# Products of scores and signs on GpSimd that wait for VectorE's mask, in a newly fitted order of work

## The chip, the cores and the metric

The kernel runs on one NeuronCore of one Trainium2 chip. The metric is the time of one execution on the device in microseconds (us). The engines are named as in the profile: PE is TensorE, DVE is VectorE, ACT is ScalarE, POOL is GpSimd, SP is SyncE, which issues the transfers.

## What is computed

A top-32 attention (8 batches, 8 heads, 576 tokens, head size 64) is followed by a layer of three products with a maximum over them and an output product (4608 tokens, 512 to 768 to 512), all in float32:

```python
scores = scale * np.matmul(q, k.transpose(0, 1, 3, 2))
kth = np.partition(scores, -top_k, axis=-1)[..., -top_k:-top_k + 1]
mask = scores >= kth
scores = np.where(mask, scores, -1000000000.0)
scores = scores - np.max(scores, axis=-1, keepdims=True)
attn = np.exp(scores)
attn = attn / (np.sum(attn, axis=-1, keepdims=True) + 1e-09)
attn_out = np.matmul(attn, v)
x = attn_out.transpose(0, 2, 1, 3).reshape(B * S, H * D)
h = np.maximum(np.maximum(x @ w1, x @ w2), x @ w3)
out = h @ w_out
```

## The kernel before

**Attention.** It goes by 144 units, each 128 queries for a pair of heads (t = 0 and 1), so that most steps come twice a unit, 288 times in all. PE makes the scores (`qk`, L508) and ACT moves them to SBUF (`evac`, L516, tile `ssb`, 128x576 for each t). To find the 32nd largest score of a row, DVE takes the eight largest of seven parts of it (`sweep`, L525), and the steps of `pivot` (L539 to L557) make from these a bound Q close to it; between them POOL turns a copy over (`negate`, L531). ACT writes the sign of Q minus score into a tile `w` and counts (`sign`, L564). POOL multiplies scores by these signs in place (`window`, L569, called the product below), DVE takes the eight largest of the result (`below`, L573), and POOL and DVE pick the threshold from the count (`place` L580 and L582, `leave` L586, `pick` L591). The mask on DVE (`mask`, L614) compares scores with the threshold and subtracts, reading `ssb` twice and writing it, and ACT takes the exponential (`expo`, L623). POOL and DVE make the inverse sum (`denominator` L629, `inverse` L633), ACT widens it (`widen`, L638), PE turns the result (`turn`, L664 to L669), ACT moves it (`turned`, L681), PE multiplies by the values (`values`, L700), and DVE, ACT and POOL scale the sums and split them into a high and a low half-precision part (`scaled_x` L710, `high_x` L724, `low_x` L728). These are x, the input of the MLP.

**The MLP.** It runs by spans of tokens: two a batch (0 to 256 and 256 to 576), three in the first. For each span and each of six blocks f, PE makes three sums (`layer`, L757, 12 matmuls each), ACT scales the first (L764), DVE takes the running maximum for the other two (`largest`, L766), ACT and POOL split it (L769, L772), and PE makes the output from all blocks (`layer2`, L817). Before that, the weights are loaded, decoded on DVE (L254 to L260), and cut into high and low parts by PE and ACT (`cut`, L325 to L334); the scale `rises` (L305) is ready when all of w1 to w3 have been seen.

**What sets the order.** Each engine works through its own list of instructions in the order in which the program issues them. That order is made by `in_order` (lines 71 to 131) at build time. Every step is a `Piece` with an engine, a cost, the pieces it needs, and a rank (its unit's number plus an offset by its kind, from the table `OFFSETS`). MLP steps are a second list, `fill`, which PE takes up when no ranked piece can start sooner, within limits of patience (`PATIENCE`) and of keeping PE in one mode (`SWITCH`, `STICK`; the modes are "rows" for `qk`, "columns" for `values`, none for the rest). Pieces marked `alone` (mask, fourth pivot step, weight decoding) share something with POOL: the planner puts them and POOL's pieces apart by its own clock:

```python
if x.alone:
    t = max(t, free["POOL"] + LOCK_A)
elif x.engine == "POOL":
    t = max(t, shut[0] + LOCK_B)
```

On the chip nothing keeps mask and product apart: the product's own needs are the sign and the buffer.

Of the kernel before, what the change touches and what calls it, by code (L numbers as in the profile page):

```python
# [14 lines left out]
ALU = mybir.AluOpType  # L15
# [9 lines left out]
NSSB = 5  # L25
NWB = 6
PMB = 2
GAP = 67.0
NEAR = 182.0
SWITCH = 100.0  # L30
STICK = 204.0
WINDOW = 150
LEAD = 49.1
LOCK_A = -150.0
LOCK_B = -100.0
OFFSETS = {'E0': -2.08, 'E1': -11.9, 'E2': 1.81, 'N': -19.09, 'T0': 7.0, 'T1': 7.99, 'T2': 7.02, 'Y': -1.5, 'Z': -8.28, 'd':
# [9 lines left out]
RANK_M = -20.0  # L46
LATE = {'PE': 160.0, 'DVE': 85.0, 'ACT': 100.0, 'POOL': 40.0, 'SP': 2000.0}

# [82 lines left out]
        left -= 1  # L131


PATIENCE = {'PE': 162, 'DVE': 131, 'ACT': 0, 'POOL': 85, 'SP': 0}


@with_exitstack
def kernel(ctx, tc, q, k, v, moe_w1, moe_w2, moe_w3, moe_w_out, out):
    nc = tc.nc
    B, NP, _, S = q.shape  # L140
    D = v.shape[-1]
    P = 128
    C = S // 64
    NU = S // P
    DM, DF = moe_w1.shape
    DO = moe_w_out.shape[1]
    KC = DM // P
# [63 lines left out]
    CUTS = {DF: DF // 2, DO: DO}  # L211
# [144 lines left out]
    lows = {}  # L356
# [47 lines left out]
    wo_scaled, wi_scaled = [], []  # L404
# [156 lines left out]
    def sign(n, t):  # L561

        d = st[n]
        nc.scalar.activation(d["w"][t], d["ssb"][t], AF.Sign, bias=d["Q"][:, t, 0:1], scale=-1.0, accum_out=d["cnt"][:, t:t + 1])  # L564

    def window(n, t):

        d = st[n]
        nc.gpsimd.tensor_tensor(d["w"][t], d["ssb"][t], d["w"][t], ALU.mult)  # L569

    def below(n, t):
        d = st[n]
# [37 lines left out]
    def mask(n, t):  # L610

        d = st[n]
        ss = d["ssb"][t]
        nc.vector.scalar_tensor_tensor(ss, ss, d["kth"][:, t:t + 1], ss, ALU.is_lt, ALU.subtract,  # L614
                                       accum_out=d["lost"][:, t:t + 1])

    def expo(n, t):
        d = st[n]
# [115 lines left out]
    def mlp(b, first, spans, tiles, alone, needs, rank):  # L734
# [39 lines left out]
        for c0, c1 in spans:  # L774
# [3 lines left out]
            for f in range(FC):  # L778
                box, prev, before = {}, None, []
                for i in range(3):  # L780
                    rel = []
                    for kcs in ((0, 1), (2, 3)):
                        x = add("PE", 6 * max(0.434 * w, 64.0), lambda i=i, f=f, kcs=kcs, c0=c0, c1=c1, box=box: layer(i, f, kcs, c0, c1, box),
                                [*needs, *(lows[i * KC + kc, f * P // CUTS[DF] * CUTS[DF]] for kc in range(KC) if lows)],
                                [("m", rel)] if kcs[0] == 0 else [])
                    now = []
                    y = add("DVE" if i else "ACT", 85 + 1.2 * w if i else 125 + 0.97 * w, lambda i=i, w=w, box=box: largest(i, w, box),
                            [x, *prev] if i else [x, *wi_scaled], [("h1", now)])
                    rel.append(y)
                    if i:  # L790
                        before.append(y)
                    before, prev = now, [y]
# [362 lines left out]
```

## Time and profile before

| | us |
|---|---|
| median of 3 runs (1251.45 to 1253.36) | 1251.83 |
| profiled execution, its own time | 1251.33 |
| span of the profiled execution | 1249.5 |
| outside the span | 1.8 |
| PE busy, share of the span | 1158.7, 93% |
| DVE busy | 1141.2, 91% |
| ACT busy | 1036.4, 83% |
| POOL busy | 866.0, 69% |
| mean granted PE clock | 0.976 |

The page gives busy time by engine and the chain of work that ended last; windows give the same by stretch, which separates the start (weights are decoded, little MLP work can run), the long middle, and the end (only MLP work is left). A granted clock of 1.00 is 2.4 GHz, 0.5 is 1.2 GHz.

### The profile page before, as it was taken

Reading aid. Unit: us, or ns where it says so; the run is one execution under the profiler, and the core shown is the slowest. Engines: PE = TensorE matmul, PEld = TensorE weight load, DVE = VectorE, ACT = ScalarE, POOL = GpSimd, SP = SyncE. Lnnn points to the kernel's source line nnn. Section 1 sums busy time; section 2 is a strip of 40 time slices with the busy share of each in tenths; the row PEclk is TensorE's granted clock in tenths of the full one; section 3 lists DMA queues with packets and bytes.
Section 4 is the critical chain, followed back from the end, with each engine's and each line's share of the span. In section 5 each row is a group of like instructions: output and inputs, shape, how many; then the busy total and the mean of one; then the engine's idle time right before and its main releaser. Section 6 shows DMA issues by size and latency. Waiting matters only on the chain.

```text
span 1249.5 us, 30550 instructions
## 1 busy us (share of the span) xinstructions
PE 1158.7 (93%) x9891; PEld 839.8 (67%) x9891; DVE 1141.2 (91%) x5547; ACT 1036.4 (83%) x2406; POOL 866.0 (69%) x1293
## 2 busy tenths in 40 slices
PE   4677789998999999999999999999899999999997
PEld 2355568775776757676777768666676768776764
DVE  8999898999999999999999999999999999999511
ACT  3688899898789998899889998898888988998621
POOL 5456687876677787777787778767777777877410
PEclk9788899999899999999999999999899999999999
DMA  8440111100111011100111021101011010000000
GB/s 329 130 139 1 56 40 48 39 28 23 36 40 47 11 55 28 58 11 20 47 48 39 11 64 40 37 11 39 29 39 47 11 47 19 13 7 2 18 18 29
DMA packets 33864, 54.74 MB, mean 44 GB/s; under 512 B 12960, under 2 KB 12960, under 8 KB 33696
## 3 DMA queue, kind: packets, MB, share of 16 engines
q1 hardware_dynamic: 33696, 52.71, 13.5%
q8 instruction: 80, 1.31, 0.4%
q14 instruction: 88, 0.72, 0.2%
HBM read 43.25 MB, written 9.44 MB: 42 GB/s over the span
## 4 chain that ended last, share of the span: by engine, by line
PE 61%; DVE 27%; ACT 8%; issue 2%; POOL 1%; DMA 0%; ACTq 0%; DVEq 0%; POOLq 0%
PE m L757 26%; PE tr L700 9%; PE s L508 9%; PE tr L669 7%; DVE L L525 7%; PE m L817 6%; DVE ssb L614 5%; DVE Q L573 4%; ACT pm L623 2%; ACT w L564 2%; PE tr L664 2%; DVE h L766 1%; DVE z L554 1%; ACT ssb L516 1%; ACT pT L681 1%
## 5 line engine op out<-in xcount | busy, mean ns | idle before, releaser
L569 POOL TENSOR_TENSOR w<-ssb,w 128x576 f32<-128x576 f32 x288 | 432.0, 1506 | 62.0 <-ACT w L564 58.8
L757 PE MATMUL m<-xh,wall 128*128 128x256 f16 (+3 forms) x2448 | 438.4, 279 | 5.8 <-DVE h L766 3.2
L757 PEld LDWEIGHTS <-wall 128*128 128x128 f16 x3672 | 347.3, 98 | 82.5 <-issue 13.5
L757 PE MATMUL m<-xl,wall 128*128 128x256 f16 (+3 forms) x1224 | 339.0, 279 | 0.0
L525 DVE MAX8 L<-ssb 128x8 f32<-128x82 f32 (+1 forms) x2016 | 316.7, 228 | 2.2 <-ACT ssb L516 2.1
L623 ACT ACTIVATE pm<-ssb,nb 128x576 f32<-128x576 f32 x288 | 224.1, 780 | 49.6 <-DVE ssb L614 49.3
L614 DVE SCALAR_TENSOR_TENSOR ssb<-ssb,kth 128x576 f32<-128x576 f32 x288 | 257.6, 910 | 0.1
L681 ACT COPY pT<-tr 128x512 f32<-128x512 f32 (+1 forms) x432 | 217.7, 514 | 28.3 <-PE tr L666 17.9
L564 ACT ACTIVATE w<-ssb,Q 128x576 f32<-128x576 f32 x288 | 223.4, 778 | 15.7 <-DVE Q L557 14.1
L573 DVE MAX8 Q<-w 128x8 f32<-128x576 f32 x288 | 214.3, 748 | 3.7 <-POOL w L569 3.4
L669 PE MATMUL tr<-ident,pm 128*128 128x128 f32 x1152 | 179.7, 282 | 24.0 <-ACT pm L623 14.3
L508 PE MATMUL s<-kT,qT 64*128 64x288 f32 x1920 | 176.5, 320 | 19.2 <-ACT ssb L516 8.7
L700 PE MATMUL tr<-pT,vt 128*64 128x256 f32 (+2 forms) x2000 | 180.8, 331 | 2.2 <-ACT s L195 1.1
L508 PEld LDWEIGHTS s<-kT,qT 64*128 64x128 f32 x1920 | 139.6, 194 | 62.6 <-ACT ssb L516 22.5
L669 PEld LDWEIGHTS tr<-ident,pm 128*128 128x128 f32 x1152 | 131.1, 142 | 69.2 <-ACT pm L623 29.9
L516 ACT ACTIVATE ssb<-s 128x1152 f32<-128x1152 f32 x144 | 163.2, 1134 | 11.4 <-PE s L508 10.7
L700 PEld LDWEIGHTS tr<-pT,vt 128*64 128x64 f32 x2000 | 112.3, 140 | 63.1 <-issue 20.8
L766 DVE SCALAR_TENSOR_TENSOR h<-m,rises,h 128x256 f32<-128x256 f32 (+3 forms) x204 | 100.2, 491 | 53.6 <-PE m L757 51.4
L772 POOL TENSOR_TENSOR hl<-h,hh 128x256 f16<-128x256 f32 (+3 forms) x102 | 82.8, 811 | 74.8 <-ACT hh L769 73.1
L817 PE MATMUL m<-wall,hh 128*128 128x512 f16 x432 | 128.5, 379 | 0.1
L629 POOL TENSOR_SCALAR den<-sums 128x2 f32<-128x2 f32 x144 | 39.4, 273 | 83.1 <-ACT pm L623 73.5
L817 PE MATMUL m<-wall,hl 128*128 128x512 f16 x216 | 81.9, 379 | 0.0
(116 smaller groups left out, 1505.8 us busy)
## 6 DMA issues: line engine op xcount, KB each, us to landing
raw<-in_k_dram SPq DMA_DIRECT2D x36, 288.0 KB, 2.8
raw<-in_q_dram SPq DMA_DIRECT2D x36, 256.0 KB, 2.8
vt<-in_v_dram SPq DMA_DIRECT2D x32, 256.0 KB, 2.8
out_dram<-ob SPq DMA_DIRECT2D x32, 256.0 KB, 2.0
wall<-in_moe_w_dram SPq DMA_DIRECT2D x8, 768.0 KB, 6.5
wall<-in_moe_w_out_dram SPq DMA_DIRECT2D x3, 512.0 KB, 6.0
raw<-in_q_dram SPq DMA_DIRECT2D x36, 32.0 KB, 2.6
vt<-in_v_dram SPq DMA_DIRECT2D x64, 16.0 KB, 2.4
```

The source lines that it names most:

```text
L508: nc.tensor.matmul(s[:, h, i, :HALF], qT[sl, qa, c0:c0 + P], kT[sl, ka, i * HALF:(i + 1) * HALF], start=(n_ == 0 and a == 0), stop=(n_ == ...
L525: nc.vector.max(d["L"][:, t, g, :], d["ssb"][t][:, g * S // G:(g + 1) * S // G])
L564: nc.scalar.activation(d["w"][t], d["ssb"][t], AF.Sign, bias=d["Q"][:, t, 0:1], scale=-1.0, accum_out=d["cnt"][:, t:t + 1])
L569: nc.gpsimd.tensor_tensor(d["w"][t], d["ssb"][t], d["w"][t], ALU.mult)
L573: nc.vector.max(d["Q"][:, t, 1:NW], d["w"][t])
L614: nc.vector.scalar_tensor_tensor(ss, ss, d["kth"][:, t:t + 1], ss, ALU.is_lt, ALU.subtract, accum_out=d["lost"][:, t:t + 1])
L623: nc.scalar.activation(d["pm"][:, t], d["ssb"][t], AF.Exp, bias=d["nb"][:, t:t + 1], scale=-1.0 / SHRINK, accum_out=d["sums"][:, t:t + 1])
L669: nc.tensor.transpose(pt[:, j * P:(j + 1) * P], pm[:, i, 64 * i + j * P:64 * i + (j + 1) * P], ident)
L681: nc.scalar.copy(pT[:, 512 * i:512 * i + m] if i < 2 else pT[:, 8 * P:10 * P], pt[:, :m])
L700: nc.tensor.matmul(xp[64 * h:64 * h + 64, to], vt[:, 4 * h + i if i < 4 else 8 + h, :], keys, start=(i == 0), stop=(i == 4))
L757: nc.tensor.matmul(box["ps", i][:, :c1 - c0], a, bb[:, kc, c0:c1], start=(kc == 0 and k == 0), stop=(kc == KC - 1 and k == 2))
L817: nc.tensor.matmul(box["po"][:n], a[:, f, cs], bb, start=(f == 0 and k == 0), stop=(f == FC - 1 and k == 2))
```

## The change

**The wait.** `mask` notes its instruction in a list `masks`, and the next product that is issued takes it out and gets a dependency on it: POOL may start that product only when that mask is done. A second product behind the same mask gets none of its own, but stands behind the first in POOL's list. A product with no mask issued since the last product gets nothing.

**The order.** The planner's constants, the table of offsets and the patience of PE, ACT and POOL have other values, and PE's `layer` steps are told to need the scales of w1 to w3 (`wi_scaled`), which until now only ACT's step behind them needed. What each engine executes is the same but for its order.

```diff
-GAP = 67.0
-NEAR = 182.0
+GAP = 68.0
+NEAR = 181.0
 SWITCH = 100.0
-STICK = 204.0
+STICK = 72.0
 WINDOW = 150
-LEAD = 49.1
+LEAD = 47.8
...
-OFFSETS = {'E0': -2.08, 'E1': -11.9, 'E2': 1.81, 'N': -19.09, 'T0': 7.0, 'T1': 7.99, 'T2': 7.02, 'Y': -1.5, 'Z': -8.28, 'd':
+OFFSETS = {'E0': -2.38, 'E1': -11.42, 'E2': 2.15, 'N': -20.8, 'T0': 6.58, 'T1': 7.44, 'T2': 6.61, 'Y': -5.44, 'Z': -11.1, 'd':
...
-PATIENCE = {'PE': 162, 'DVE': 131, 'ACT': 0, 'POOL': 85, 'SP': 0}
+PATIENCE = {'PE': 114, 'DVE': 131, 'ACT': 29, 'POOL': 100, 'SP': 0}
...
+    masks = []
+    behind = mybir.DependencyInfo(mybir.DependencyClass.Sync, mybir.DependencyReason.ANTI)
+
     def window(n, t):
 
         d = st[n]
-        nc.gpsimd.tensor_tensor(d["w"][t], d["ssb"][t], d["w"][t], ALU.mult)
+        x = nc.gpsimd.tensor_tensor(d["w"][t], d["ssb"][t], d["w"][t], ALU.mult)
+        if masks:
+            tc.add_manual_dep(x.ins, masks.pop(), behind, reason="one port")
...
-        nc.vector.scalar_tensor_tensor(ss, ss, d["kth"][:, t:t + 1], ss, ALU.is_lt, ALU.subtract,
-                                       accum_out=d["lost"][:, t:t + 1])
+        x = nc.vector.scalar_tensor_tensor(ss, ss, d["kth"][:, t:t + 1], ss, ALU.is_lt, ALU.subtract,
+                                           accum_out=d["lost"][:, t:t + 1])
+        masks[:] = [x.ins.name]
...
-                                [*needs, *(lows[i * KC + kc, f * P // CUTS[DF] * CUTS[DF]] for kc in range(KC) if lows)],
+                                [*needs, *wi_scaled, *(lows[i * KC + kc, f * P // CUTS[DF] * CUTS[DF]] for kc in range(KC) if lows)],
```

Three places of the order follow. Lines of the changed kernel are up to six higher: product L572, mask L619, maximum L772.

First, POOL's list near the end of the attention, with the engines whose semaphores each instruction waits for. Before:

```order
L586 TENSOR_TENSOR oh<-oh,Q 128x18 [waits DVE_49,Pool_49]
L569 TENSOR_TENSOR w<-ssb,w 128x576 [waits Activation_49]
L728 TENSOR_TENSOR xl<-xs,xh 128x256 [waits Activation_49]
L569 TENSOR_TENSOR w<-ssb,w 128x576
L531 TENSOR_SCALAR nA<-L 128x56 [waits DVE_49]
L580 TENSOR_TENSOR oh<-spots,cnt 128x18
L582 TENSOR_SCALAR oh<-oh 128x18 [waits Pool_49]
L569 TENSOR_TENSOR w<-ssb,w 128x576 [waits Activation_49]
L586 TENSOR_TENSOR oh<-oh,Q 128x18 [waits DVE_49,Pool_49]
L569 TENSOR_TENSOR w<-ssb,w 128x576 [waits Activation_49]
L629 TENSOR_SCALAR den<-sums 128x2 [waits Activation_49]
```

With the change:

```order
L591 TENSOR_TENSOR oh<-oh,Q 128x18 [waits DVE_49,Pool_49]
L572 TENSOR_TENSOR w<-ssb,w 128x576 [waits Activation_49]
L734 TENSOR_TENSOR xl<-xs,xh 128x256 [waits Activation_49]
L572 TENSOR_TENSOR w<-ssb,w 128x576
L585 TENSOR_TENSOR oh<-spots,cnt 128x18
L587 TENSOR_SCALAR oh<-oh 128x18 [waits Pool_49]
L531 TENSOR_SCALAR nA<-L 128x56 [waits DVE_49]
L572 TENSOR_TENSOR w<-ssb,w 128x576 [waits DVE_49,Activation_49]
L591 TENSOR_TENSOR oh<-oh,Q 128x18 [waits DVE_49,Pool_49]
L572 TENSOR_TENSOR w<-ssb,w 128x576 [waits Activation_49]
L635 TENSOR_SCALAR den<-sums 128x2 [waits Activation_49]
```

One of the four products here has a wait for DVE beside that for ACT. Of all 288 products 111 show one; before, none did. In the order in which the program issues all work, 151 products come as the first behind a mask and are given the new dependency; where no wait is shown, an earlier one of POOL covers it. In the order of before there are 141 such places.

Second, DVE's list from the last `scaled_x` of the attention (`xs`) to the scales of the output (`so`). Before:

```order
L710 SCALAR_TENSOR_TENSOR xs<-tr,down_v,pT 128x128
L766 SCALAR_TENSOR_TENSOR h_20864<-m,rises,h_20849 128x256
L1069 TENSOR_REDUCE flag<-tr 1x1
L1071 CAST flag_i<-flag 1x1
L766 SCALAR_TENSOR_TENSOR h_20879<-m,rises,h_20864 128x256
L766 SCALAR_TENSOR_TENSOR h_20911<-m,rises,h_20896 128x256
L766 SCALAR_TENSOR_TENSOR h_20926<-m,rises,h_20911 128x256
L766 SCALAR_TENSOR_TENSOR h_20958<-m,rises,h_20943 128x256
L766 SCALAR_TENSOR_TENSOR h_20973<-m,rises,h_20958 128x256
L766 SCALAR_TENSOR_TENSOR h_21005<-m,rises,h_20990 128x256
L766 SCALAR_TENSOR_TENSOR h_21017<-m,rises,h_21005 128x256
L802 TENSOR_SCALAR so_21020<-back_wi,back_wo,back_v 128x1
```

With the change:

```order
L716 SCALAR_TENSOR_TENSOR xs<-tr,down_v,pT 128x128
L772 SCALAR_TENSOR_TENSOR h_20911<-m,rises,h_20871 128x256
L772 SCALAR_TENSOR_TENSOR h_20926<-m,rises,h_20911 128x256
L1075 TENSOR_REDUCE flag<-tr 1x1
L1077 CAST flag_i<-flag 1x1
L772 SCALAR_TENSOR_TENSOR h_20958<-m,rises,h_20943 128x256
L772 SCALAR_TENSOR_TENSOR h_20973<-m,rises,h_20958 128x256
L772 SCALAR_TENSOR_TENSOR h_21005<-m,rises,h_20990 128x256
L772 SCALAR_TENSOR_TENSOR h_21017<-m,rises,h_21005 128x256
L808 TENSOR_SCALAR so_21020<-back_wi,back_wo,back_v 128x1
```

Behind the last `xs` stand six maxima of 256 columns instead of eight. On PE, 90 `layer` matmuls of 256 columns stand behind the last `values`, and 138 did before; the rest of the end is the same.

Third, DVE's list from the scale `rises` to the first maximum of the MLP. Before:

```order
L305 TENSOR_SCALAR rises<-backs,down_wi 128x3
L554 SCALAR_TENSOR_TENSOR z<-n_1231,b_1_121 128x18
L543 MAX n_1350<-nA 128x8 x2
L545 TENSOR_REDUCE nb<-nA 128x2
L557 TENSOR_REDUCE Q<-z 128x2
L573 MAX Q<-w 128x8
L549 MATCH_REPLACE nR<-n_1350,nA 128x28 x2
L551 MAX n_1350<-nR 128x8 x2
L591 TENSOR_REDUCE kth<-oh 128x2
L539 MAX b_2_122<-L 128x8 x2
L525 MAX L<-ssb 128x8 x8
L766 SCALAR_TENSOR_TENSOR h_1411<-m,rises,h_1355 128x128
```

With the change:

```order
L305 TENSOR_SCALAR rises<-backs,down_wi 128x3
L619 SCALAR_TENSOR_TENSOR ssb,lost<-ssb,kth 128x576
L578 MAX Q<-w 128x8
L549 MATCH_REPLACE nR<-n_1407,nA 128x28 x2
L551 MAX n_1407<-nR 128x8 x2
L539 MAX b_0_120<-L 128x8 x2
L525 MAX L<-ssb 128x8 x8
L639 RECIPROCAL rs<-den 128x2
L554 SCALAR_TENSOR_TENSOR z<-n_1407,b_0_120 128x18
L257 SCALAR_TENSOR_TENSOR ob<-wall,ob 128x512
L772 SCALAR_TENSOR_TENSOR h_1571<-m,rises,h_1504 128x128
```

The first maximum stands behind 16 masks of the attention instead of 12, the ninth behind 34 instead of 26, the 25th behind 56 instead of 50 and the 49th behind 82 instead of 81. Changes of PE's mode over the whole list are 427 instead of 422.

## Rows read from the trace of the kernel before

**Rows 1.** The profile's page, part 1: span, busy time, share and instructions by engine.
```profile
span 1249.5 us, 30550 instructions
PE 1158.7 (93%) x9891; PEld 839.8 (67%) x9891; DVE 1141.2 (91%) x5547; ACT 1036.4 (83%) x2406; POOL 866.0 (69%) x1293
```

**Rows 2.** Windows: stretch, length, then busy us and (instructions) by engine, clock, DMA.
```profile
core 0: us, PE busy (x) PEld busy (x) DVE busy (x) ACT busy (x) POOL busy (x), PEclk, DMA share, GB/s
...
200.00:1175.00 975.00, 945.64 (x8262) 693.85 (x8259) 944.40 (x4698) 866.83 (x2030) 734.21 (x1102) 0.99 0.11 32
300.00:325.00 25.00, 17.25 (x119) 11.35 (x119) 23.07 (x124) 19.43 (x45) 19.79 (x30) 0.80 0.15 47
870.00:886.00 16.00, 11.60 (x70) 6.94 (x68) 14.33 (x71) 12.97 (x30) 12.76 (x18) 0.79 0.33 108
100.00:150.00 50.00, 37.71 (x263) 25.05 (x261) 46.52 (x216) 41.84 (x95) 33.59 (x46) 0.83 0.12 35
0.00:200.00 200.00, 145.82 (x1131) 99.80 (x1132) 184.56 (x822) 155.16 (x349) 123.02 (x180) 0.90 0.34 113
...
1173.40:1249.50 76.10, 68.78 (x513) 47.37 (x513) 13.43 (x34) 15.40 (x31) 9.21 (x13) 0.99 0.06 19
```

**Rows 3.** The page, part 4: the chain that ended last, by engine.
```profile
PE 61%; DVE 27%; ACT 8%; issue 2%; POOL 1%; DMA 0%; ACTq 0%; DVEq 0%; POOLq 0%
```

**Rows 4.** The page, part 5: product (L569) and mask (L614), busy and mean, idle before.
```profile
L569 POOL TENSOR_TENSOR w<-ssb,w 128x576 f32<-128x576 f32 x288 | 432.0, 1506 | 62.0 <-ACT w L564 58.8
L614 DVE SCALAR_TENSOR_TENSOR ssb<-ssb,kth 128x576 f32<-128x576 f32 x288 | 257.6, 910 | 0.1
```

**Rows 5.** One line's instructions: count, shortest/median/longest ns, first and last start.
```profile
L614 DVE SCALAR_TENSOR_TENSOR ssb<-ssb,kth x288: 789/810/2126, 35.3 to 1170.5; 128x576 f32<-128x576 f32 x144
...
L569 POOL TENSOR_TENSOR w<-ssb,w x288: 1395/1416/2057, 30.0 to 1166.0; 128x576 f32<-128x576 f32 x144
```

**Rows 6.** Timeline (start, length): products that got in ahead, first and last of 12.
```profile
159.99 1.41 POOL L569 TENSOR_TENSOR w<-ssb,w 128x576 f32<-128x576 f32 x1
...
160.15 1.87 DVE L614 SCALAR_TENSOR_TENSOR ssb<-ssb,kth 128x576 f32<-128x576 f32 x1
...
162.06 0.78 ACT L623 ACTIVATE pm<-ssb,nb 128x576 f32<-128x576 f32 x1 [1.20 <-DVE ssb L614]
...
1054.38 1.97 POOL L569 TENSOR_TENSOR w<-ssb,w 128x576 f32<-128x576 f32 x1
...
1055.01 1.96 DVE L614 SCALAR_TENSOR_TENSOR ssb<-ssb,kth 128x576 f32<-128x576 f32 x1
```

**Rows 7.** Timeline: products held behind a mask, first and last of 44.
```profile
119.08 0.81 DVE L614 SCALAR_TENSOR_TENSOR ssb<-ssb,kth 128x576 f32<-128x576 f32 x1
...
119.29 1.89 POOL L569 TENSOR_TENSOR w<-ssb,w 128x576 f32<-128x576 f32 x1
...
1155.96 0.81 DVE L614 SCALAR_TENSOR_TENSOR ssb<-ssb,kth 128x576 f32<-128x576 f32 x1
...
1156.07 1.96 POOL L569 TENSOR_TENSOR w<-ssb,w 128x576 f32<-128x576 f32 x1
```

**Rows 8.** Timeline: VectorE's last pivot step and the sign that waits for it.
```profile
603.70 0.16 DVE L557 TENSOR_REDUCE Q<-z 128x2 f32<-128x18 f32 x1
...
603.96 0.78 ACT L564 ACTIVATE w<-ssb,Q 128x576 f32<-128x576 f32 x1 [0.62 <-DVE Q L557]
```

**Rows 9.** Waits: who waited for whom, us in total, times, longest.
```profile
PEld tr L700 <- issue: 20.8, 78, 0.8
...
PEld s L508 <- issue: 11.5, 44, 0.4
...
DVE Q L573 <- POOL w L569: 3.4, 8, 1.1
```

**Rows 10.** The chain in order of time: MLP products behind the attention.
```profile
1180.43 13.10 PE m L757 x120
```

**Rows 11.** One line's instructions: the maximum of the MLP (L766) on VectorE.
```profile
L766 DVE SCALAR_TENSOR_TENSOR h<-m,rises,h x204: 326/484/552, 104.6 to 1230.7; 128x256 f32<-128x256 f32 x48, 128x320 f32<-128x320 f32 x42, 128x128 f32<-128x128 f32 x6, 128x192 f32<-128x192 f32 x6
```

18 rows, old and new, of the table OFFSETS are left out of this document.

## Prediction

> **What bounds the kernel now.** I read the page's busy shares first, then the same by stretch, then the chain that ended last, then mask and product by themselves. The profiled execution took 1251.33 us, of which the span is 1249.5 [rows 1]; the other 1.8 us I leave as they are. It lies 0.5 us below the median of the runs, 1251.83. PE and DVE are both nearly full: 93% and 91% of the span [rows 1], but from 200 to 1175 us PE is busy 945.6 of 975 us and DVE 944.4 [rows 2]. The reader is to see that neither alone sets the time there. The chain agrees: PE has 61% of it, DVE 27%, POOL 1% [rows 3]. The first 200 us are different. PE is busy 145.8 us [rows 2] at a mean granted clock of 0.90, so some of it ran at the lower level of 1.2 GHz; DVE is busy 184.6 us. At the end, from 1173.4 us on, PE works through the last batch's MLP with DVE busy for 13.4 of 76.1 us [rows 2]. Since PE's work is the same before and after, the time changes by what PE loses: about 54 us idle in the first 200 us (200 less 145.8) and 29.4 in the middle (975 less 945.6).
>
> **Mask against product.** Most masks take 810 ns, the longest 2126; most products 1416, the longest 2057 [rows 5]. The means are 910 and 1506 [rows 4], so 288 masks lose about 288 x 0.100 = 28.8 us and 288 products about 25.9 us. The timeline shows how. Where the product starts first, the mask lasts until the product has ended: product at 159.99 for 1.41 us, mask from 160.15 for 1.87 us [rows 6]. Where the mask starts first, the product is stretched: mask from 119.08 for 0.81, product from 119.29 for 1.89 [rows 7]. One always stands still for the other. For each first product behind a mask in program order I looked at both in this trace: of 141 pairs the mask had ended in 82; the product was already held by a mask in 44; it got in ahead in 12; three are neither.
>
> **The wait, part by part.** (1) In the 12 cases the mask would run first and take about 0.81 us instead of 1.77 to 2.04. The first saves 1.87 - 0.81 = 1.06, the last 1.96 - 0.81 = 1.15 [rows 5, 6]; all 12 together 14.1 us of DVE. What is queued behind the mask on DVE, and ACT's exponential that waits for it (it idled 1.20 us for the first one [rows 6]), comes as much earlier. The remaining half of the 28.8 us stays: there a product that the program issues ahead of the mask, or other work of POOL, is in the way, and the change adds no wait for those. What this saves at the end lies between nothing and all 14.1 us. I take DVE's share of the chain, 27% [rows 3]: **-3.8 us**.
> (2) POOL pays. The 12 products start later by the mask's 0.81 us and what it started behind them (160.15 + 0.81 - 159.99 = 0.97 for the first, 1.44 for the last [rows 6]); 11.4 us in all. The 44 held ones lose a head start: the first ends 1.29 us after its mask (119.29 + 1.89 less 119.08 + 0.81), the last 1.26 [rows 7], both less than the 1.416 of a free one. With a wait the product starts only when the semaphore has come; another step from DVE to an engine took 603.96 - 603.86 = 0.10 us [rows 8]. So 44 x (1.416 + 0.10 - 1.28) = 10.4 us. Behind the waiting product stand POOL's `negate`, `denominator` and `place`, for which DVE waits. But POOL idles 31% of the span [rows 1], and DVE waited for products only 3.4 us in 8 places [rows 9]. The bounds are nothing and the whole 21.8 us; by POOL's 1% of the chain [rows 3] I take **+0.2 us**.
>
> The Trainium skill, in "SBUF — State Buffer" (Who interferes with whom), says that a VectorE instruction with two SBUF inputs and a GpSimd instruction that reads SBUF share a port, and that the order of issue decides which of the two blocks. That this trace agrees on, 1.87 us for the mask in one order and 1.89 for the product in the other, speaks for the first rival below rather than for my sum: by it the wait only chooses who stands still.
>
> **The order, part by part.** (3) The end. Behind the last `values` 138 matmuls of 256 columns stood, now 90. At 13.10 us for 120 [rows 10] the 48 are worth 5.2 us of PE's last stretch. They have to be done earlier. If the attention's end moves back by as much, nothing is won; if they fill PE's idle time in the middle, 29.4 us [rows 2], all is. Both engines are equally full there, so I take half: **-2.6 us**.
> (4) Mode changes on PE, five more in the whole list. The waits put down to "issue" at such places are 20.8 us for 78 and 11.5 for 44 [rows 9], 0.27 each: at most 1.3; I take **+1.0 us**.
> (5) The start. The ninth maximum of the MLP stands behind 34 masks instead of 26. From 35.3 to 1170.5 us there are 288 masks [rows 5], one in 3.94 us, so the fill is behind by 8 x 3.94 = 31.5 us of attention; by the 49th maximum it has caught up to one mask. Where PE has little fill, from 100 to 150 us, it idles 12.3 of 50 us, 25% [rows 2], so the lag could cost 31.5 x 0.25 = 7.8 us. On the other side, PE now runs out of MLP work later: from 300 to 325 us it idles 7.75 us at a clock of 0.80 [rows 2], the time between two spans of the first batch, and with fill held back less of this hole is left. Lag and hole are the same size with opposite signs: **0**, with -7.8 and +7.8 as ends.
> PE's `layer` steps standing behind `rises` costs nothing: what PE did before the scale was there had to stay in PSUM until ACT and DVE had it, and the first maximum came at 104.6 us [rows 11]. Without that cover it is part of (5).
>
> The sum: -3.8 + 0.2 - 2.6 + 1.0 + 0 = -5.2. 1251.3 - 5.2 = **1246.1 us**.
>
> **Rivals.** *The waits only change sides.* DVE gains 14.1 us and POOL loses 21.8, and a product lies in the same unit's path (product, eight largest, threshold, mask, exponential, turn), so what comes earlier in one unit comes later in the next. For it: POOL is idle before products only for ACT's signs, 58.8 us [rows 4], so its list does run close behind. Against: 8 waits of DVE for a product in all [rows 9]. Or the 111 waits are mostly met when they are reached, as in 82 of 141 pairs. Then -3.8 and -2.6 fall away: 1251.3 + 1.2, or 1252.5.
>
> *Slower: the MLP starts late.* The first maximum stands behind 16 masks instead of 12, the ninth behind 34. PE has no other work than attention while DVE, busy 184.6 of 200 us [rows 2], is the slow one there. If the hole at 300 to 325 us stays as well, the lag of 7.8 us is lost, and the end gives nothing back: 1251.3 - 3.8 + 0.2 + 1.0 + 7.8 = 1256.5 us. It decides if PE idles over 6 us more in the first 250 us without idling less after.
>
> *Much faster.* The masks lie on the path with all 14.1 us, since DVE is 97% busy in the middle [rows 2] and each unit's steps follow each other; and the end's 5.2 us come off whole: 1251.3 - 14.1 - 5.2 + 1.2 = 1233.2 us. Against: PE is as full as DVE, and has 29.4 us to give there in all.
>
> **How the numbers follow.** A measurement of this kernel can tell about 0.2%, 2.5 us, from no change. I give the forecast 0.45, the exchange 0.22, the late start 0.19, the large gain 0.14. The forecast's own range, from half the lag lost to half the hole won, is 1242 to 1250. The whole range goes from the middle of the large gain, 1235, to a little over the late start, 1258; the far ends of the bounds (all of POOL's 21.8 us on the path, or every gain at once) are left out as less than 2 in 10. Faster by over 0.2%: the large gain and most of the forecast, 0.14 + 0.42 = 0.56. Within it: most of the exchange, 0.19, and 0.02 of the forecast, 0.21. Slower: the late start and the rest, 0.23.
>
> **What the profile will show.** Right: the mean of the mask falls from 910 to about 910 - 14.1/288, or 860 ns, its longest ones go; products longer than 1.45 us nearly vanish (the mean falls by up to 25.9/288 = 90 ns), and a new wait of POOL's product on DVE's mask appears, some 20 us; PE's last stretch is about 71 us instead of 76.1; PE's idle time from 200 us on falls below 29 us. Wrong: if POOL's waits on masks come to far over 40 us and DVE begins to wait for `negate`, `denominator` or products; if PE's idle time of the first 250 us grows by more than the middle gains; or if masks stay at 0.9 us on average because other work of POOL takes the products' place.

## The result and the profile after

The changed kernel takes 1213.26 us (median of 4 runs, 1212.89 to 1214.68) against 1252.59 in runs beside it: a ratio of 0.9688, with a 95% interval from 0.9671 to 0.9705, so 39 us or 3.1% faster. The forecast had 1246.1 and a range from 1235 to 1258. The direction was right; the size was not, and not even the case of the large gain (1233.2) reached so far.

The profiled execution of the changed kernel has this span and these busy times on the page, to be set beside [rows 1]:

```profile
span 1211.5 us, 30557 instructions
...
PE 1147.8 (95%) x9891; PEld 836.2 (69%) x9891; DVE 1119.2 (92%) x5547; ACT 1035.3 (85%) x2406; POOL 853.9 (70%) x1293
```

The span is 38.0 us shorter. PE's busy time fell by 10.9 us and DVE's by 22.0. PE does the same work; that its busy time fell fits the mean granted clock, which is 0.984 and was 0.976, so that less of the span ran at 1.2 GHz. The remaining 27.1 us are idle time of PE that is gone. The windows show where (stretch, length, then busy time and instructions by engine), of the changed kernel and then of before:

```profile
core 0: us, PE busy (x) PEld busy (x) DVE busy (x) ACT busy (x) POOL busy (x), PEclk, DMA share, GB/s
...
0.00:200.00 200.00, 147.04 (x1164) 100.71 (x1164) 188.76 (x877) 161.74 (x366) 129.55 (x193) 0.91 0.34 111
200.00:1100.00 900.00, 896.31 (x7935) 663.31 (x7935) 883.13 (x4492) 825.43 (x1928) 688.17 (x1044) 1.00 0.12 34
300.00:350.00 50.00, 50.00 (x484) 39.82 (x481) 49.27 (x246) 43.06 (x102) 39.68 (x60) 1.00 0.17 49
```

```profile
200.00:1100.00 900.00, 870.82 (x7662) 640.52 (x7660) 876.38 (x4374) 801.84 (x1876) 681.33 (x1021) 0.99 0.11 33
...
300.00:350.00 50.00, 42.17 (x357) 32.79 (x357) 46.07 (x229) 40.76 (x95) 35.68 (x56) 0.90 0.10 30
```

From 200 to 1100 us PE is busy 896.3 of 900 us, where it was 870.8; almost nothing is left to fill. From 300 to 350 us it had idled 7.8 us at a clock of 0.90 and now does not idle at all. In the first 200 us it is busy 147.0 us, against 145.8 [rows 2].

Product and mask, on the page and with shortest, median and longest duration:

```profile
L572 POOL TENSOR_TENSOR w<-ssb,w 128x576 f32<-128x576 f32 x288 | 407.1, 1418 | 120.2 <-ACT w L564 51.0
...
L619 DVE SCALAR_TENSOR_TENSOR ssb<-ssb,kth 128x576 f32<-128x576 f32 x288 | 247.4, 871 | 0.1
```

```profile
L619 DVE SCALAR_TENSOR_TENSOR ssb<-ssb,kth x288: 791/810/2159, 44.5 to 1135.7; 128x576 f32<-128x576 f32 x144
...
L572 POOL TENSOR_TENSOR w<-ssb,w x288: 1395/1412/1811, 35.4 to 1130.4; 128x576 f32<-128x576 f32 x144
```

The product's mean fell from 1506 [rows 4] to 1418 ns: products are hardly stretched any more. The mask's fell from 910 to 871; 39 ns x 288 are 11.2 us. Masks of 2 us still occur where a product or a subtraction that the program issues ahead of the mask is in the way; the longest, 2.159 us, stood behind a subtraction of POOL (L469). The masks are only half of what DVE saves. Most of the rest is the fourth pivot step, which also has two inputs in SBUF, before and now:

```profile
L554 DVE SCALAR_TENSOR_TENSOR z<-n,b 128x18 f32<-128x18 f32 x144 | 44.9, 313 | 0.3
...
L554 DVE SCALAR_TENSOR_TENSOR z<-n,b 128x18 f32<-128x18 f32 x144 | 36.3, 252 | 0.0
```

Among POOL's waits a new one stands beside that for ACT's sign:

```profile
POOL w L572 <- ACT w L564: 51.0, 39, 5.5
...
POOL w L572 <- DVE ssb L619: 44.7, 42, 2.5
```

Two examples of it on the timeline, each with a sign that ACT had made before:

```profile
103.65 0.77 ACT L564 ACTIVATE w<-ssb,Q 128x576 f32<-128x576 f32 x1
...
104.02 0.81 DVE L619 SCALAR_TENSOR_TENSOR ssb<-ssb,kth 128x576 f32<-128x576 f32 x1
...
104.98 1.41 POOL L572 TENSOR_TENSOR w<-ssb,w 128x576 f32<-128x576 f32 x1 [1.42 <-DVE ssb L619]
```

```profile
601.42 0.78 ACT L564 ACTIVATE w<-ssb,Q 128x576 f32<-128x576 f32 x1
...
602.04 0.74 POOL L531 TENSOR_SCALAR nA<-L 128x56 f32<-128x56 f32 x1
...
603.29 0.80 DVE L619 SCALAR_TENSOR_TENSOR ssb<-ssb,kth 128x576 f32<-128x576 f32 x1
...
604.18 1.42 POOL L572 TENSOR_TENSOR w<-ssb,w 128x576 f32<-128x576 f32 x1 [1.40 <-DVE ssb L619]
```

In the first the mask ends at 104.83 and the product starts 0.15 us later. The product's sign was ready only at 104.42, when the mask was already running: without the wait this product would have begun behind the mask and been held, as in [rows 7]. The second is the kind that the change is meant for. Both signs of the unit were done by 602.20, and POOL was free at 602.78, half a microsecond before the mask began: without the wait the product would have been first, and the mask would have stood still until it was done, as in [rows 6]. Of the 42 waits above, 8 are of this second kind; in the other 34 the mask was already running when the product could have started.

### The profile page after: what moved, and what is told of

It is laid out like the page before. It is cut to its first block, busy times and chain, and to the rows that moved or that the text cites. A ratio compares the mean times of both kernels' runs of the same rounds, so it can differ in the third digit from the quotient of the medians.

```text
span 1211.5 us, 30557 instructions
## 1 busy us (share of the span) xinstructions
PE 1147.8 (95%) x9891; PEld 836.2 (69%) x9891; DVE 1119.2 (92%) x5547; ACT 1035.3 (85%) x2406; POOL 853.9 (70%) x1293
## 3 DMA queue, kind: packets, MB, share of 16 engines
q1 hardware_dynamic: 33696, 52.71, 14.3%
## 5 line engine op out<-in xcount | busy, mean ns | idle before, releaser
L572 POOL TENSOR_TENSOR w<-ssb,w 128x576 f32<-128x576 f32 x288 | 407.1, 1418 | 120.2 <-ACT w L564 51.0
L619 DVE SCALAR_TENSOR_TENSOR ssb<-ssb,kth 128x576 f32<-128x576 f32 x288 | 247.4, 871 | 0.1
L508 PE MATMUL s<-kT,qT 64*128 64x288 f32 x1920 | 172.7, 315 | 16.2 <-ACT ssb L516 9.5
L508 PEld LDWEIGHTS s<-kT,qT 64*128 64x128 f32 x1920 | 136.5, 190 | 60.5 <-ACT ssb L516 21.7
L772 DVE SCALAR_TENSOR_TENSOR h<-m,rises,h 128x256 f32<-128x256 f32 (+3 forms) x204 | 100.0, 490 | 45.5 <-PE m L763 43.1
L778 POOL TENSOR_TENSOR hl<-h,hh 128x256 f16<-128x256 f32 (+3 forms) x102 | 80.1, 785 | 62.2 <-ACT hh L775 61.2
```

Source lines behind the costliest of these rows:

```text
L508: nc.tensor.matmul(s[:, h, i, :HALF], qT[sl, qa, c0:c0 + P], kT[sl, ka, i * HALF:(i + 1) * HALF], start=(n_ == 0 and a == 0), stop=(n_ == ...
L572: x = nc.gpsimd.tensor_tensor(d["w"][t], d["ssb"][t], d["w"][t], ALU.mult)
L619: x = nc.vector.scalar_tensor_tensor(ss, ss, d["kth"][:, t:t + 1], ss, ALU.is_lt, ALU.subtract, accum_out=d["lost"][:, t:t + 1])
```

## Experiments

All are timed against the kernel before. Each of the first three undoes or does one part of the change. Wait and order can be separated exactly, since the planner that makes the order does not know of the wait: in the first two runs every engine's instructions come in the same order as in the kernel that was edited.

**The new order without the wait.** The edit to the changed kernel:

```diff
         x = nc.gpsimd.tensor_tensor(d["w"][t], d["ssb"][t], d["w"][t], ALU.mult)
-        if masks:
-            tc.add_manual_dep(x.ins, masks.pop(), behind, reason="one port")
```

> The new order of all work, without the product's wait for the mask; every engine's list is that of the changed kernel. Theory A (the wait carries most of the 39 us, because it makes the chip follow the planned order of mask and product): at most 10 us faster than before, some 1243 us, with masks of 2 us and stretched products back and PE idle 20 us or more from 200 us on. Theory B (the order carries it, the wait gives the 4 us or so that were forecast): 1217 to 1221 us, PE idle under 8 us from 200 us on. Theory C (they need each other): in between, 1225 to 1240.

Measured: 1230.36 us, ratio 0.9821 (0.9799 to 0.9843). Its windows, and the mask on its page:

```profile
0.00:200.00 200.00, 145.80 (x1162) 100.29 (x1163) 189.41 (x870) 161.18 (x365) 132.31 (x193) 0.91 0.34 111
200.00:1100.00 900.00, 885.79 (x7798) 650.64 (x7796) 882.76 (x4409) 812.65 (x1896) 692.76 (x1027) 1.00 0.12 34
300.00:350.00 50.00, 49.83 (x483) 39.40 (x483) 49.35 (x253) 43.05 (x100) 40.76 (x59) 1.00 0.19 54
...
L617 DVE SCALAR_TENSOR_TENSOR ssb<-ssb,kth 128x576 f32<-128x576 f32 x288 | 262.2, 923 | 0.1
```

The order alone gives 21.5 us. The hole at 300 to 350 us is closed by it, without the wait. Masks are worse than before (923 ns). The 17.1 us from here to the changed kernel are the wait's in the new order. Theory C fits the time; neither part is small.

**The old order with the wait alone.** The edit is the change's hunks in `window` and `mask` and nothing else.

> The old order with the wait alone; every engine's list is that of before. Theory A: 1220 to 1230 us, PE idle from 200 us on down from 29 to under 12 us. Theory B: 1246 to 1250 us, the mean of the mask near 860 ns, PE idle from 200 us on still over 20 us. Theory C: 1240 to 1250, with POOL's waits pushing the unchanged order out of step.

Measured: 1241.44 us, ratio 0.9916 (0.9899 to 0.9933). Windows, mask, and POOL's wait for it:

```profile
200.00:1100.00 900.00, 878.18 (x7755) 647.64 (x7754) 873.47 (x4422) 812.30 (x1900) 673.95 (x1031) 0.99 0.12 33
300.00:350.00 50.00, 43.12 (x367) 33.45 (x365) 45.17 (x223) 41.60 (x96) 35.38 (x54) 0.90 0.10 30
...
L619 DVE SCALAR_TENSOR_TENSOR ssb<-ssb,kth 128x576 f32<-128x576 f32 x288 | 247.1, 873 | 0.1
...
POOL w L572 <- DVE ssb L619: 28.5, 27, 2.7
```

The wait alone gives 10.4 us, which is in theory C's range and in no other. Added to the order's 21.5 it makes 31.9 of the 39.3 us; the rest comes only with both. Masks fell from 910 to 873 ns, 10.7 us in all, and the time by about the same. The hole at 300 to 350 us stays as it was: PE is busy 43.1 of 50 us, and was 42.2. So the two parts do different things. The start of the masks in the traces shows it (us; the 144 units have 288 masks):

| mask | before | wait alone | order alone | both |
|---|---|---|---|---|
| 32nd | 184.2 | 185.2 | 176.4 | 175.7 |
| 72nd | 349.7 | 347.3 | 333.4 | 330.1 |
| 144th | 627.2 | 623.0 | 608.7 | 603.3 |
| 288th | 1170.5 | 1160.7 | 1152.2 | 1135.7 |

The order wins 16.3 of its 18.3 us before the 72nd mask, 7.8 of them before the 32nd; the wait wins its 9.8 us (16.5 in the new order) bit by bit over the whole attention, over half of it behind the 144th mask.

**Only the planner's need of the scales.** The edit to the kernel before:

```diff
-                                [*needs, *(lows[i * KC + kc, f * P // CUTS[DF] * CUTS[DF]] for kc in range(KC) if lows)],
+                                [*needs, *wi_scaled, *(lows[i * KC + kc, f * P // CUTS[DF] * CUTS[DF]] for kc in range(KC) if lows)],
```

> Before, with nothing changed but that the planner lets PE's first MLP sums need the scales of w1 to w3; the planner makes another order from that. If PE's early sums held PSUM while they waited for the scale and cost time at the start, PE idles some 5 us less in the first 200 us and the time falls by 3 to 8 us. If that cost nothing, the time stays within 4 us of before, and what it moves is the chance of another order.

Measured: 1229.65 us, ratio 0.9825 (0.9805 to 0.9845), as much as the whole new order gave and far outside both expected ranges.

```profile
0.00:200.00 200.00, 142.98 (x1133) 98.34 (x1134) 186.25 (x845) 157.48 (x356) 126.19 (x184) 0.91 0.34 111
200.00:1100.00 900.00, 887.26 (x7847) 652.98 (x7847) 882.37 (x4460) 816.87 (x1910) 701.46 (x1040) 1.00 0.12 34
300.00:350.00 50.00, 46.93 (x449) 35.88 (x446) 48.67 (x240) 46.17 (x108) 43.32 (x63) 1.00 0.12 37
```

The gain is not at the start, as was expected if there was one: PE is busy 143.0 us of the first 200, less than before. It is after 200 us: 887.3 instead of 870.8. The 72nd mask starts at 338.5, the last at 1148.9. So the need works by the other order that the planner makes of it, and not by what the early sums cost.

**That need and the wait, with the constants and offsets of before.**

> Before with the planner's new need of the scales and with the wait, all constants and offsets of before. The need alone gave -22 us and the wait alone -10. Theory D (the new constants give nothing beyond the need): 1212 to 1220 us, as the changed kernel. Theory E (the new constants are what the wait needs to give more): 1220 to 1230.

Measured: 1225.99 us, ratio 0.9783 (0.9752 to 0.9814).

```profile
0.00:200.00 200.00, 143.51 (x1111) 99.07 (x1113) 184.79 (x834) 155.94 (x349) 123.87 (x183) 0.90 0.34 111
200.00:1100.00 900.00, 893.44 (x7902) 658.63 (x7899) 878.01 (x4482) 821.98 (x1923) 695.15 (x1047) 1.00 0.12 34
```

The time is in theory E's range: the new constants and offsets give another 12.7 us with the wait, while without it they gave nothing beyond the need (1230.36 against 1229.65). How far this is the fit of the order to the wait and how far the scatter of orders, which the next runs show, was not tried.

**A small step of one constant, at both ends.** The kernel before with `GAP = 68.0` for 67.0, and the changed kernel with 67.0 for 68.0.

> Before with one constant of the planner changed by 1.5% (GAP 68 for 67), which makes another order of much the same kind, without the need and without the wait. Theory F (the need of the scales is a mechanism: early MLP sums that cannot be emptied hold up the start): the time stays within 5 us of before. Theory G (any new order of before falls some 10 to 20 us one way or the other, and the need's -22 us is one such draw): it differs from before by over 8 us.

> The changed kernel with GAP 67 for 68, the same small step the other way. It shows how far a change of the plan of no meaning moves the time with the wait in place: within 4 us if the wait keeps the chip close to the plan; over 8 us if the order of the change is a lucky one.

Measured: 1243.12 us, ratio 0.9913 (0.9880 to 0.9946), for the first, and 1218.75, ratio 0.9729 (0.9697 to 0.9761), for the second. Windows of the first, then of the second:

```profile
0.00:200.00 200.00, 138.61 (x1102) 95.66 (x1103) 185.82 (x833) 153.32 (x345) 126.83 (x183) 0.90 0.34 111
200.00:1100.00 900.00, 883.26 (x7777) 650.74 (x7775) 870.92 (x4414) 810.04 (x1901) 695.92 (x1028) 0.99 0.12 34
300.00:350.00 50.00, 48.14 (x426) 37.60 (x426) 48.36 (x241) 44.44 (x105) 40.50 (x60) 0.97 0.13 37
```

```profile
0.00:200.00 200.00, 146.94 (x1171) 100.95 (x1172) 189.58 (x883) 162.70 (x369) 130.97 (x194) 0.91 0.34 111
200.00:1100.00 900.00, 889.79 (x7889) 658.12 (x7889) 883.39 (x4466) 821.18 (x1918) 682.81 (x1039) 1.00 0.12 34
```

A step without meaning makes the old kernel 9.7 us faster and the changed one 5.5 us slower. Orders of the same kind thus scatter by 5 to 10 us; theory G holds as far as that, and the second lies between the two cases that were expected. In the first one the hole at 300 to 350 us is nearly closed too (48.1 us busy), at the cost of the start (138.6 us busy in 200).

**The changed kernel with the old table of offsets.**

> The changed kernel with the offsets of before; wait, need and the other constants are those of the change. If the table of offsets is fitted to the wait, 1222 to 1235 us; if the table is worth nothing by itself, 1210 to 1220.

Measured: 1230.11 us, ratio 0.9820 (0.9788 to 0.9852).

```profile
0.00:200.00 200.00, 132.50 (x1016) 89.59 (x1017) 188.75 (x836) 152.75 (x343) 123.06 (x182) 0.88 0.33 111
200.00:1100.00 900.00, 894.50 (x7967) 661.65 (x7964) 874.40 (x4453) 819.77 (x1919) 679.90 (x1039) 1.00 0.12 34
```

The time is in the range expected if the table is fitted to the wait, but the place is another. The middle is almost as full as in the changed kernel (894.5 us, there 896.3). Most of the 17 us are lost at the start: PE is busy 132.5 us of the first 200 instead of 147.0. The table was not tried without the wait.

**The MLP held back at the start.** In the kernel before, the first batch's sums need the masks of a later unit, 12 or 16:

```diff
-                                [*needs, *(lows[i * KC + kc, f * P // CUTS[DF] * CUTS[DF]] for kc in range(KC) if lows)],
+                                [*needs, *([of[12]["m", 1]] if b == 0 else []), *(lows[i * KC + kc, f * P // CUTS[DF] * CUTS[DF]] for kc in range(KC) if lows)],
```

> Before, without wait and without the need of the scales; the planner lets the first batch's MLP sums begin only when the masks of unit 12 are done, so the first stands behind 26 masks instead of 12. Theory H (holding the MLP back at the start lets the attention get ahead, and then PE does not run out of MLP work near 300 to 350 us): 1225 to 1240 us, PE's idle time from 200 us on below 20 us of 29, none of it lost before 200 us. Theory G (orders scatter by 10 us and the lag has nothing to do with it): within 1240 to 1262, PE idle at 300 to 350 us as before. The forecast's view of the lag as a cost: 1252 to 1260, PE idle in the first 200 us up by 5 us or more.

> The same, held back to unit 16 (first sum behind 34 masks). Theory H: again 10 to 25 us faster than before, or less where PE now idles at the start (over 60 us of the first 200). Theory G: within 1240 to 1262, on either side of the run with unit 12.

Measured: 1242.55 us, ratio 0.9923 (0.9906 to 0.9941), with unit 12; 1234.66, ratio 0.9852 (0.9835 to 0.9868), with unit 16. Windows of the one, then of the other:

```profile
0.00:200.00 200.00, 139.52 (x1042) 93.30 (x1044) 185.22 (x829) 156.41 (x350) 125.69 (x183) 0.89 0.33 111
200.00:1100.00 900.00, 882.61 (x7854) 651.42 (x7851) 879.76 (x4413) 808.78 (x1896) 687.77 (x1028) 1.00 0.12 34
300.00:350.00 50.00, 49.27 (x470) 39.87 (x469) 49.04 (x228) 44.58 (x106) 43.28 (x62) 1.00 0.13 37
```

```profile
0.00:200.00 200.00, 140.67 (x946) 93.25 (x946) 184.78 (x826) 152.78 (x337) 122.47 (x178) 0.84 0.34 111
200.00:1100.00 900.00, 888.42 (x7969) 658.17 (x7966) 881.39 (x4464) 820.19 (x1928) 700.18 (x1044) 1.00 0.12 34
300.00:350.00 50.00, 49.27 (x478) 40.05 (x475) 48.86 (x246) 44.81 (x107) 41.65 (x60) 1.00 0.13 36
```

The two profiled executions took the same time, 1238.5 us, 4 us below the median of the one run and 4 above that of the other. The first MLP matmul starts at 164.2 and 191.6 us instead of 99.8. The first 200 us do lose PE work (139.5 and 140.7 us busy, before 145.8), but the hole at 300 to 350 us closes in both (49.3), and the time falls. The 720th `layer` matmul starts at 336.3 and 342.4, and before at 334.2: the fill has almost caught up by then, while the 72nd mask starts 9.8 and 13.9 us earlier.

What the hole is can be read from the traces. The first batch has 648 `layer` matmuls. Between the last of them and the first of the second batch PE starts no `layer` matmul (starts in us):

| | last of batch 1 | first of batch 2 | between | 60th mask |
|---|---|---|---|---|
| before | 293.6 | 325.6 | 32.0 | 302.0 |
| wait alone | 293.0 | 323.2 | 30.2 | 299.8 |
| order alone | 302.0 | 311.9 | 9.9 | 287.8 |
| both | 298.7 | 308.6 | 9.9 | 284.5 |
| need of the scales | 302.8 | 316.2 | 13.4 | 290.7 |
| `GAP` 68 | 305.7 | 320.0 | 14.3 | 294.4 |
| unit 12 | 311.2 | 321.4 | 10.2 | 286.4 |
| unit 16 | 321.5 | 331.4 | 9.9 | 293.6 |

In every other order than that of before the first batch ends later, and the gap shrinks to less than half. What theory H foresaw is seen in both runs: held back, the same sums fill time that was empty, and the attention is ahead by the 60th mask. Its numbers are borne out in part, and with orders that scatter by 10 us the time of the unit 12 run alone would show nothing. The unit 16 run lies in its range; the unit 12 run, at 1242.55, misses it (1225 to 1240) and falls into theory G's, though with the hole closed; and PE's work before 200 us, of which none was to be lost, is 5 to 6 us less. Nor is a late first sum needed for it: with `GAP` 68 the MLP begins at 98.7 us and with the need at 103.0, and the gap closes nearly as far.

**More waits.** The changed kernel, in which the next product waits for the fourth pivot step (L554) too; in which POOL's other large subtractions take the wait for the mask as well; and with both.

```diff
...
-            nc.vector.scalar_tensor_tensor(z, d["n8"].rearrange("p t i j -> p t (i j)")[:, :, 4 * G - 24:4 * G - 15], -SHRINK, b9s[n % 3], ALU.mult,
-                                           ALU.min)
+            x = nc.vector.scalar_tensor_tensor(z, d["n8"].rearrange("p t i j -> p t (i j)")[:, :, 4 * G - 24:4 * G - 15], -SHRINK, b9s[n % 3], ALU.mult,
+                                               ALU.min)
+            masks[:] = [x.ins.name]
```

> The changed kernel, in which the next product also waits for the fourth pivot step of VectorE (L554), the other instruction of DVE with two inputs in SBUF. It lost 11.9 us against POOL in the changed kernel, 8.9 of them to products. If DVE's lost time is worth what it was in the change (about 14 us of masks for 10 to 17 us), 1206 to 1210 us; if these waits cost POOL as much as they give, 1211 to 1218.

> The changed kernel, in which the other large subtractions of POOL (L469, L734, L778) take the wait for the mask as well when they come first behind one. They cost the masks some 8 us and hold up none of the search. If a wait is worth it wherever the two meet, 1207 to 1212 us; if POOL's list is now what runs late, 1214 to 1222.

> The changed kernel with the waits of both runs before it: for the fourth pivot step too, and of POOL's other subtractions too. Each alone left PE no emptier than 4 us from 200 us on. If PE is the bound there now, 1209 to 1214 us, no more than 3 us below the changed kernel, although DVE loses some 6 us less than in it.

Measured: 1213.47 us, ratio 0.9686 (0.9670 to 0.9702); 1212.25, ratio 0.9677 (0.9661 to 0.9693); and 1213.71, ratio 0.9691 (0.9673 to 0.9708). None differs from the changed kernel by more than a measurement tells. The first one's middle and busy times:

```profile
200.00:1100.00 900.00, 897.59 (x7954) 664.47 (x7954) 882.44 (x4505) 827.97 (x1936) 691.60 (x1045) 1.00 0.12 34
...
PE 1146.8 (95%) x9891; PEld 835.9 (69%) x9891; DVE 1116.4 (92%) x5547; ACT 1035.2 (86%) x2406; POOL 855.0 (71%) x1293
```

DVE has only 2.8 us less to do than in the changed kernel, in the second run 1.7 and with both 1.2 instead of the 6 expected; the pivot step's mean fell only from 252 to 231 ns. The reading by which the time would come to 1206 to 1210 us fell. PE's middle, busy 897.6 of 900 us, leaves nothing to win there, so PE as the bound fits all three; that DVE's time is worth nothing more is not shown, since 1 to 3 us of it are about what a measurement can tell. The second run's 1212.25 lies just outside both of its expected ranges.

**The price of a microsecond of DVE and of POOL.** The kernel before, with one small step done twice in each unit into a tile that nobody reads: `pick`'s reduction on DVE, `denominator` on POOL. The order stays as it was.

```diff
+        nc.vector.tensor_reduce(sm.tile([P, 2], F32, name="again"), d["oh"], AX.X, ALU.max)
         nc.vector.tensor_reduce(d["kth"], d["oh"], AX.X, ALU.max)
```

> Before, with one reduction of 18 elements a row done twice in each unit (144 more on DVE, into a tile that nobody reads); every engine's order stays as it was. At 0.09 to 0.16 us each DVE has 13 to 23 us more work. By the forecast's price (DVE's 27% of the chain) the time rises by 3.5 to 6 us; if a microsecond of DVE is a microsecond of the end, as the runs with and without the wait say, by 13 to 23.

> Before, with the small step ahead of the inverse sum done twice in each unit on POOL (144 more of 0.19 us, 28 us of POOL's time, into a tile that nobody reads); order as it was. If POOL has room for it, as the forecast took from its 31% idle and its 1% of the chain, the time rises by at most 3 us; if POOL's list runs close behind, by 10 us or more.

Measured: 1264.85 us, ratio 1.0108 (1.0086 to 1.0131), and 1262.48, ratio 1.0077 (1.0060 to 1.0095). Busy times and the mask of the first; busy times of the second and DVE's wait for the doubled step:

```profile
PE 1160.6 (92%) x9891; PEld 839.4 (67%) x9891; DVE 1158.0 (92%) x5691; ACT 1035.8 (82%) x2406; POOL 863.2 (69%) x1293
...
L615 DVE SCALAR_TENSOR_TENSOR ssb<-ssb,kth 128x576 f32<-128x576 f32 x288 | 264.5, 934 | 0.1
```

```profile
PE 1162.0 (92%) x9891; PEld 839.2 (67%) x9891; DVE 1150.4 (91%) x5547; ACT 1036.3 (82%) x2406; POOL 898.9 (71%) x1437
...
DVE rs L634 <- POOL den L630: 10.4, 33, 1.0
```

DVE's busy time rose by 16.8 us (6.9 of them are masks, 934 ns instead of 910, that met POOL more often), and the time by 12.5: 0.7 us for one. The four runs spread from 1259.9 to 1268.47, and the profiled one is the fastest; by its span, 8.5 us longer, it is 0.5. That is under the 13 to 23 us of the one reading and well over the 3.5 to 6 of the forecast's price. POOL's rose by 32.9 us and the time by 10.1: 0.3 for one. Two things can cost it: DVE waited 10.4 us for the step that was doubled, and DVE's own busy time rose by 9.2 us (its masks to 925 ns), as it met POOL more often. They were not separated. The wait before was:

```profile
DVE rs L633 <- POOL den L629: 3.7, 5, 1.7
```

Either way POOL did not have the room that the forecast took.

## Why the prediction was wrong

**Part (1), the price of DVE's time, was mis-sized.** The mechanism was right: masks that got stuck behind a product no longer do. Of the 14.1 us that the 12 pairs were to save, the wait saves 10.7 net in the old order: the mask that took 1.87 us [rows 6] takes 0.80, but some others now meet other work of POOL. I multiplied by DVE's 27% of the chain, -3.8 us. The wait alone gave 10.4 us for 10.7 of mask time, in the new order 17.1 for 15.0 (923 - 871 ns, x 288), and doubled work on DVE cost 0.5 to 0.7 for one. A share of one chain is not a rate of exchange. The table of the masks shows the gain growing from unit to unit: what DVE loses anywhere moves the later units, and PE idles with it (from 200 to 1100 us 29.2 us before, 21.8 with the wait alone). Not all of the wait's gain need be DVE's time, since products are no longer stretched either.

**Part (2), POOL's cost, was right in kind.** The products' stretch is gone and waits of 44.7 us took its place, over twice the 20 us foreseen; yet DVE's wait for products stayed small (2.5 us, before 3.4 [rows 9]). That POOL's time costs next to nothing (+0.2) was not right in general, as 0.3 for one in the last run shows. The rival that the waits only change sides fell: it gave 1252.5, and the wait alone took 1241.44. The rule of the Trainium skill's "SBUF — State Buffer" (Who interferes with whom), that the order of issue decides which of the two blocks, agrees with both traces: a mask of 1.87 us behind a product [rows 6], and in the changed kernel one of 2.159 us behind a subtraction that is issued ahead of it. But a wait that moves the standstill to the engine with more idle time is worth something: POOL stands still for the mask, and the last mask starts 9.8 us earlier, 16.5 in the new order.

**Part (5), the start, is the step that failed.** I read the lag of the MLP behind the attention as a loss of up to 7.8 us, against a hole that might close for the same, and set their sum to 0. Measured, the order alone gives 21.5 us, where parts (3) to (5) came to -1.6 in all, and the 72nd mask is 16.3 us earlier. Lag and hole are not two terms of opposite sign. The MLP work that PE does early is taken from a stock that is short later: before, the first batch's sums ran out at 293.6 us and the next batch's began at 325.6. Held back, they fill part of that gap, and the attention gets ahead: with units 12 and 16 the 280th of the 2016 `sweep` steps starts at 189.6 and 192.8 us instead of 194.6, and the 60th mask at 286.4 and 293.6 instead of 302.0. Even a start 92 us later (unit 16) made the kernel 17.8 us faster. The rival of the late start (1256.5) fell by the same runs. In the change itself the first MLP matmul starts only 6 us later (106.0), and 7.8 of the 16.3 us are won before the 32nd mask, where the runs with units 12 and 16 win nothing; so it is shown that holding the sums back can close the gap and save time, and not how much of the order's own gain comes by it.

In part (5) I also put PE's need of the scales at nothing. By itself it made the old kernel 22.2 us faster, by the order that the planner made from it: the gap between the batches fell from 32.0 to 13.4 us. That one more need can move the whole order was left out.

**Part (3), the end, came as computed.** The last `values` end with this row before and with the second one now:

```profile
1176.86 1.39 PE L700 MATMUL tr<-pT,vt 128*64 128x64 f32 x40
```

```profile
1144.33 1.39 PE L706 MATMUL tr<-pT,vt 128*64 128x64 f32 x40
```

From there to the end of the span it is 71.2 us before (1249.5 - 1178.25) and 65.8 now (1211.5 - 1145.72), 5.4 us less; 5.2 were forecast. It was half counted, because I feared that the attention's end would move back by as much; it moved ahead.

**The check by the profile.** Of the signs named, the stretched products nearly vanished (1418 ns), the new wait came, PE's last stretch is shorter and its middle has idle time far under 29 us: from 200 to 1100 us 3.7. The mask's mean, 871, came near the 860 given, but the longest masks, which were to go, did not (2159 ns, before 2126). That PE had only 29.4 us to give in the middle was right, and it gave nearly all of them; what I left out is that PE's busy time falls too, by 10.9 us at a clock of 0.984 instead of 0.976.

**What stays open.** Of the order's gain, how much is the start's lag and how much another property of it: a step of 1.5% in one constant gave 9.7 us too, and all reorderings that I ran of the old kernel were faster than it, so that the kernel before lay at the slow end of orders of its kind. The new order closes the gap between the batches while it also gets ahead at the start; which constants do which was not tried, nor the new constants without the need of the scales.

## What to carry to other kernels

Where two engines are both nearly full and feed each other, price a microsecond by an experiment that adds one, not by an engine's share of the chain that ended last. When two engines take turns at something and one of them has idle time, let that one wait by a semaphore, so that the standstill falls where it is cheaper. Work that fills gaps is a stock: before counting a later start of it as a loss, look for the place where it runs out.

## What was not expected of the hardware

A product that is held behind a mask ends 1.26 to 1.29 us after it [rows 7], less than the 1.41 that one takes by itself; one that waits for the mask's semaphore starts 0.15 us after the mask's end and takes the full 1.41 us. The wait thus costs POOL 0.27 to 0.30 us for each product that would have been held anyway, and it still pays. And PE's granted clock fell with the hole at 300 to 350 us: it was 0.90 in the two runs of the old order that leave the hole (before, and the wait alone, PE busy 42.2 and 43.1 us) and 1.00 in the changed kernel, which fills it. Idle time alone does not set it: with the need of the scales PE was busy 46.9 us there at 1.00, with `GAP` 68 48.1 us at 0.97.
